# Attention, first round of batch 0: scores formed a second time, transposed, in place of 128-wide transposes of the exponentials

## The chip, the core and the metric

The kernel runs on one core of one Trainium2 chip, as one launch. The metric is the time of an execution on the device. A core has five engines that run side by side, each through its own list of instructions in order: PE (TensorE, products into PSUM), DVE (VectorE), ACT (ScalarE), POOL (GpSimd) and SP (SyncE, which here issues every DMA). They wait for each other through semaphores.

## The reference, cut to what matters

Sixteen pairs of heads (4 batches, 8 heads), 1152 keys and 64 values a head. Two neighbouring query rows are averaged, so 576 queries a head remain; then softmax attention, and on its output a bilinear layer in which two products of the same input are multiplied and sent through a third.

```python
q_pool = q.reshape(B, H, S // factor, factor, D).mean(axis=3)
scores = scale * np.matmul(q_pool, k.transpose(0, 1, 3, 2))
scores = scores - np.max(scores, axis=-1, keepdims=True)
attn = np.exp(scores)
attn = attn / (np.sum(attn, axis=-1, keepdims=True) + 1e-09)
attn_out = np.matmul(attn, v)
x = attn_out.transpose(0, 2, 1, 3).reshape(B * S, H * D)     # 2304 x 512
out = ((x @ w_a) * (x @ w_b)) @ w_out                        # 512 -> 1536 -> 512
```

## The kernel before

A pass takes one pair of heads (e = 0, 1) and some of their queries, in blocks of 128 queries by 1152 keys. Batch 0 goes in two rounds: first the "even" 256 queries of its four pairs (passes 0 to 3, four blocks each), then the "odd" 320 in reverse order (passes 4 to 7). Batches 1 to 3 take all 576 queries of a pair in one pass. Beside passes 0 to 3 the weights of the bilinear layer are prepared: 36 tiles are loaded, and each is taken apart into a large and a small half by ACT (`w_abs` L558, `w_tail` L577, `w_hi` L622), POOL (`w_sign` L581) and DVE (`w_join` L588, `w_lo` L626). The products of that layer (`moe_mm` L919, then `moe_o` L945) start when the first round of batch 0 is done and fill PE to the end of the program, between the blocks of later passes.

A block in passes 0 to 3, before: PE forms the scores (`qk` L682, two heads at a time in the two halves of the array's rows). DVE takes them from PSUM, negated, with their maximum (`sm_max` L717). ACT makes the exponentials with their sum (`sm_exp` L724). PE transposes them in 128x128 pieces (`tr_pe` L760) into the banks `ab0` and `ab1`, and ACT and DVE take turns to carry these to `pt` (`tr_out` L771, L773), read there as 32-bit numbers under the name `ptf`. PE multiplies with v (`pv_f` L804, two heads in the two halves of the array's columns). The reciprocal of the sum is spread by a diagonal matrix and a product with ones (`r_diag` L776, `r_wide` L780); `x_copy` L848 and `r_mul` L784 apply it. From pass 4 on a block goes another way: halves of 16 bits (`sm_hi` L737, `sm_lo` L741) and a DMA that transposes them into `pt` (L747); L838 multiplies with v.

The order of each engine's instructions is written out by hand: `ORDERS` lists the numbers of the tasks in the order in which `add` created them, one list an engine, and `Plan.order` only interleaves the five lists. The waits come from a tracker of what each instruction reads and writes in the tiles, whatever names the plan gave them.

## Time and profile before

| what | value |
|---|---|
| median of 3 runs | 839.35 us (837.95 to 842.45) |
| the profiled execution | 840.88 us, its span 839.1 us |
| busy share of the span | PE 93%, DVE 74%, ACT 69%, POOL 29% |
| mean granted TensorE clock | 0.981 |
| chain that ended last, by engine | PE 57%, DVE 2%, DMA 1% |

The span runs from the first to the last instruction. An engine is busy while an instruction runs; a clock of 1.00 is TensorE's upper level (2.4 GHz), its lower one is half of that. In a row of the timeline stand start, length, engine, line, operation, what is written and read, and in brackets the idle time before and what ended it. The length holds the tail of an instruction, under which the next one already runs, so the difference of two starts is the better measure in a dense stretch. Each 32-bit product shows as two matrix instructions (x10 is five products).

### The profile page before, as it was taken

Reading aid. Unit: us, or ns where it says so; the run is one execution under the profiler, and the core shown is the slowest. Engines: PE = TensorE matmul, PEld = TensorE weight load, DVE = VectorE, ACT = ScalarE, POOL = GpSimd, SP = SyncE. Lnnn points to the kernel's source line nnn. Section 1 sums busy time; section 2 is a strip of 40 time slices with the busy share of each in tenths; the row PEclk is TensorE's granted clock in tenths of the full one; section 3 lists DMA queues with packets and bytes.
Section 4 is the critical chain, followed back from the end, with each engine's and each line's share of the span. In section 5 each row is a group of like instructions: output and inputs, shape, how many; then the busy total and the mean of one; then the engine's idle time right before and its main releaser. Section 6 shows DMA issues by size and latency. Waiting matters only on the chain.

```text
span 839.1 us, 21333 instructions
## 1 busy us (share of the span) xinstructions
...
## 2 busy tenths in 40 slices
...
GB/s 262 208 188 204 208 144 192 211 199 196 209 212 210 195 200 189 232 173 217 192 185 211 182 206 194 164 171 173 151 127 127 127 30 128 13 26 1 27 2 25
DMA packets 316289, 132.32 MB, mean 158 GB/s; under 512 B 300832, under 2 KB 302880, under 8 KB 316192
## 3 DMA queue, kind: packets, MB, share of 16 engines
...
## 4 chain that ended last, share of the span: by engine, by line
PE 57%; DVE 2%; DMA 1%; ACT 0%; issue 0%
PE ab L919 26%; PE ab L945 15%; PE sps L685 8%; PE xps L838 8%; DMA pt<-p 1%; DVE p L741 1%; DVE s L717 1%; PE sps L682 0%; DVE g L931 0%; ACT g L926 0%; DVE o L951 0%; PE xps L496 0%; ACT p L737 0%; ACT s L724 0%; PE xps L429 0%
## 5 line engine op out<-in xcount | busy, mean ns | idle before, releaser
L919 PEld LDWEIGHTS <-wab 128*128 128x128 f16 x2592 | 252.2, 99 | 37.3 <-issue 6.3
L919 PE MATMUL ab<-xt,wab 128*128 128x256 f16 x2304 | 262.7, 274 | 2.7 <-DVE xt L881 0.9
L724 ACT ACTIVATE s<-s,st 128x1152 f32<-128x1152 f32 x144 | 179.9, 1250 | 34.5 <-DVE s L717 34.0
L939 POOL TENSOR_TENSOR gl<-g,gh 128x256 fp32r<-128x256 f32 x108 | 94.5, 880 | 358.1 <-ACT gh L936 349.7
L741 DVE SCALAR_TENSOR_TENSOR p<-s,st,p 128x1152 f16<-128x1152 f32 x128 | 181.5, 1424 | 10.0 <-ACT p L737 9.5
L737 ACT ACTIVATE p<-s,st 128x1152 f16<-128x1152 f32 x128 | 159.0, 1248 | 37.9 <-DMA pt<-p 13.3
L945 PE MATMUL ab<-wo,gh 128*128 128x512 f32 x432 | 139.8, 405 | 1.7 <-DVE g L931 1.7
L682 PE MATMUL sps<-k,q 64*128 64x512 f32 (+3 forms) x448 | 103.9, 557 | 22.6 <-DVE s L717 10.5
L926 ACT ACTIVATE g<-ab,cc 128x256 f32<-128x256 f32 (+1 forms) x144 | 55.4, 415 | 90.4 <-PE ab L919 90.3
L717 DVE TENSOR_SCALAR_CACHE_REDUCE s<-sps 128x1152 f32<-128x1152 f32 x72 | 96.7, 1350 | 25.7 <-PE sps L682 24.5
L717 DVE TENSOR_SCALAR_CACHE_REDUCE s<-sps,ksc 128x1152 f32<-128x1152 f32 x72 | 101.0, 1410 | 15.7 <-PE sps L685 15.3
L838 PE MATMUL xps<-pt,vs 128*64 128x128 f16 (+1 forms) x3888 | 109.3, 215 | 1.4 <-DMA pt<-p 1.1
L838 PEld LDWEIGHTS <-vs 128*64 128x64 f16 x3888 | 100.5, 110 | 13.5 <-issue 11.6
L931 DVE SCALAR_TENSOR_TENSOR g<-ab,cc,g 128x256 f32<-128x256 f32 (+1 forms) x144 | 55.2, 410 | 72.6 <-ACT g L926 72.6
L682 PEld LDWEIGHTS sps<-k,q 64*128 64x128 f32 (+1 forms) x448 | 48.5, 187 | 75.4 <-issue 52.4
L945 PEld LDWEIGHTS ab<-wo,gh 128*128 128x128 f32 x432 | 77.9, 188 | 20.4 <-ACT g L926 1.7
L945 PE MATMUL ab<-wo,gl 128*128 128x512 f32 x216 | 85.4, 395 | 0.0
L936 ACT ACTIVATE gh<-g 128x256 fp32r<-128x256 f32 x108 | 43.8, 411 | 54.8 <-PE ab L945 54.1
L685 PE MATMUL sps<-k,q 64*128 64x512 f16 (+3 forms) x624 | 65.5, 341 | 0.0
L685 PEld LDWEIGHTS <-q 64*128 64x128 f16 (+1 forms) x720 | 36.2, 97 | 39.6 <-issue 7.0
L581 POOL TENSOR_SCALAR xt<-xt 128x512 f16<-128x512 f32 x22 | 51.9, 2357 | 35.3 <-ACT xt L577 25.9
L419 POOL TENSOR_TENSOR q<-qraw 128x576 f32<-128x576 f32 (+2 forms) x20 | 25.0, 1250 | 92.3 <-PE sps L682 48.9
...
## 6 DMA issues: line engine op xcount, KB each, us to landing
...
```

The lines of the kernel that those rows point to most:

```text
L682: nc.tensor.matmul(out, q, k, start=True, stop=True)
L685: nc.tensor.matmul(out, q[:, hq], k[:, hk], start=(hq, hk) == (0, 0), stop=(hq, hk) == (1, 0))
L717: nc.vector.tensor_scalar(out=s_t[sbuf(i)], in0=sps[:, at:at + S], scalar1=-1.0 / 16.0 if u is None else ksc[:, u, 4:5], scalar2=None, op0 ...
L724: nc.scalar.activation(out=s, in_=s, func=AF.Exp, scale=-1.0, bias=t[:, 0:1], accum_out=t[:, 1:2])
L737: nc.scalar.activation(out=p_t[pbuf(i)][:, 0], in_=s_t[sbuf(i)], func=AF.Copy, scale=st_t[i % NST][:, 3:4])
L741: nc.vector.scalar_tensor_tensor(out=p[:, 1], in0=s, scalar=st_t[i % NST][:, 3:4], in1=p[:, 0], op0=ALU.mult, op1=ALU.subtract)
L838: nc.tensor.matmul(xps[half(e), at:at + w], vs[:, c, e, hv], pt[:, hp, c, c0:c0 + w], start=(c == 0 and n == 0), stop=(c == NCH - 1 and n ...
L919: nc.tensor.matmul(dst if t < 8 else dst.rearrange("p (b n) -> p b n", b=B), wab[:, f, 1 - m, a, c], moe_x(t, b, c), start=(n == 0), stop= ...
L926: nc.scalar.activation(out=g_t[:, f, c], in_=ab[j][:, 1, c], func=AF.Copy, scale=cc[:, b, f, 0:1])
L931: nc.vector.scalar_tensor_tensor(out=g, in0=ab[j][:, 0, c], scalar=cc[:, b, f, 1:2], in1=g, op0=ALU.mult, op1=ALU.mult)
L939: nc.gpsimd.tensor_tensor(out=gl_t[j], in0=g_t[:, f], in1=gh_t[j].bitcast(F32), op=ALU.subtract)
L945: nc.tensor.matmul(acc[u], g[:, us], wo[:, f, a], start=(first and n == 0), stop=(last and n == 2))
```

## The change

In passes 0 to 3 the blocks' scores are formed as before, but only for their maxima (`t_max`, a plain reduction). Four products with the identity lay the maxima of the 256 queries out as a row (`t_row`), which ACT copies (`t_keep`). Then the scores are formed again, transposed: keys on the partitions, 256 queries along the row, in five groups of two chunks of 128 keys (the last has one), and a second product subtracts the row of maxima (`t_s`). ACT makes the exponentials straight from PSUM into the place from which v is multiplied (`t_exp`): for passes 0 and 2 the buffers `p` and `s`, for 1 and 3 `pt`. `t_pv` multiplies with v, and by a product with ones also forms the sums, spread over the 64 rows of a head. `t_sum`, `t_rec` and `t_out` copy the sums, take their reciprocal and multiply. Diagonals, transposes and their copies are gone. `w_cc`, which scales the weights' factors, makes one instruction for four columns where there was one for each half column. All five lists of the order are new.

```diff
@@ -27,12 +27,13 @@
 P_SCALE = 2.0 ** 14
 
 REMN = 64
-N_PE, EVICT = 4, "ADADA"
+CC_F = 4
+N_PE = 4
 N_WHOLE, TWO_ROUNDS = 2, (0,)
 
 XE, XR, XO = 0, 256, 320
 
-S_AT = (0, 1408)
+S_AT, GAP = (0, 1408), 1152
 S_CUT = ((0, 512, 1024, 1152), (128, 640, 1152, 0, 128))
 TOK = 256
 
@@ -55,159 +56,154 @@
 
 ORDERS = (
     (
...
-        12, 18, 24, 26, 38, 28, 7, 30, 32, 44, 34, 35, 54, 56, 151, 58, 52, 60, 62, 157, 64, 65, 163, 177, 82, 167,
+        13, 15, 17, 19, 21, 8, 23, 133, 27, 26, 135, 31, 137, 35, 139, 30, 39, 141, 34, 38, 42, 143, 50, 253, 64, 147,
...
@@ -390,8 +387,19 @@
     kz = [z_t[2][:, 128 * j:128 * j + 128] for j in range(2)]
     kzf = [x.bitcast(F16).rearrange("p (a n) -> p a n", a=2) for x in kz]
 
-    ident, diag = g_t[:, 0, 0:128], [g_t[:, 1 + e, 0:128] for e in range(2)]
-    ptf = pt.rearrange("p a c n -> p (a c n)").bitcast(F32).rearrange("p (a c n) -> p a c n", a=2, c=NCH)
+    ident, sel = g_t[:, 0, 0:128], g_t[:, 1, 0:128]
+    mrow, rsum = [g_t[:, 2], g_t[:, 3]], g_t[:, 4]
+    GROUPS = [range(c, min(c + 2, NCH)) for c in range(0, NCH, 2)]
+    spare = [(x.rearrange("p a n -> p (a n)").bitcast(F32), [f"p{j}h", f"p{j}l"]) for j, x in enumerate(p_t)]
+    spare += [(x, [f"s{j}"]) for j, x in enumerate(s_t)]
+    spare = [(x[:, 512 * n:512 * n + 512], names) for x, names in spare for n in range(2)]
+    wide = pt.rearrange("p a c n -> p (a c n)").bitcast(F32)
+    wide = [(wide[:, 512 * n:512 * n + 512], [f"pt{j}" for j in range(NR)]) for n in range(9)]
+
+    def room(j, g, e):
+        n = 2 * g + e if g < 4 else 8
+        x, names = (spare, wide)[j][n]
+        return x[:, 256 * e:256 * e + 256] if g == 4 else x, names
     vf = [vs.rearrange("p c e h d -> p (c e h d)").bitcast(F32).rearrange("p (c n) -> p c n", c=NCH), vraw]
 
     def vbuf(p):
@@ -604,11 +613,10 @@
     def w_inv(f):
         nc.vector.reciprocal(out=wsc[:, 0, f], in_=wsc[:, 1, f])
 
-    def w_cc(f):
-        for m in range(2):
-            nc.vector.tensor_scalar(
-                out=cc[:, 0, f, m:m + 1], in0=wsc[:, 1, f, m:m + 1], scalar1=vb[:, 0, 0:1], scalar2=None, op0=ALU.mult
-            )
+    def w_cc(f0, f1):
+        nc.vector.tensor_scalar(
+            out=cc[:, 0, f0:f1], in0=wsc[:, 1, f0:f1], scalar1=vb[:, 0, 0:1], scalar2=None, op0=ALU.mult
+        )
 
     def w_dst(f, m, hl):
         return wab[:, f, m, hl] if m < 2 else wo[:, f, hl]
@@ -755,56 +763,87 @@
             out=ident, in_=ident, compare_op=ALU.not_equal, fill=1.0, base=0, pattern=[[-1, 128]], channel_multiplier=1
         )
 
-    def tr_pe(chunks, j):
...
-    def tr_out(chunks, j, on):
...
-    def r_diag(i, e):
...
-    def r_wide():
...
-    def r_mul(j, x0):
...
-    def moved(ps_, i0, u):
...
-    def pv_f(p, at, m):
...
+    def select():
+        nc.gpsimd.memset(sel, 0.0)
+        for e in range(2):
+            nc.gpsimd.memset(sel[64 * e:64 * e + 1], -1.0)
+
+    def t_max(i):
+        at = S_AT[blocks[i].head]
+        nc.vector.tensor_reduce(out=st_t[i % NST][:, 0:1], in_=sps[:, at:at + S], axis=AX.X, op=ALU.max)
+
+    def t_row(i0):
+        for r in range(2):
+            for e in range(2):
+                m = st_t[(i0 + 2 * r + e) % NST][:, 0:1]
+                nc.tensor.matmul(
+                    sps[half(e), GAP + 128 * r:GAP + 128 * r + 128], m.broadcast_to([128, 64]), ident, start=True, stop=True
+                )
+
+    def t_keep(j):
+        nc.scalar.activation(out=mrow[j], in_=sps[:, GAP:GAP + TOK], func=AF.Copy)
+
+    def t_s(ps_, j, g):
+        for n, c in enumerate(GROUPS[g]):
             for e in range(2):
                 nc.tensor.matmul(
+                    acc[e][:, TOK * n:TOK * n + TOK], kn[ps_.jk][half(e), 128 * c:128 * c + 128],
+                    qs[ps_.jq][half(e), 0:TOK], start=True, stop=False,
                 )
+            for e in range(2):
+                nc.tensor.matmul(acc[e][:, TOK * n:TOK * n + TOK], sel[half(e)], mrow[j][half(e)], start=False, stop=True)
+
+    def t_exp(j, g, e):
+        n = len(GROUPS[g])
+        nc.scalar.activation(
+            out=room(j, g, e)[0], in_=acc[e][:, 0:TOK * n], func=AF.Exp, scale=1.0 / 16.0
+        )
+
+    def t_pv(p, j, g):
+        at = [room(j, g, e)[0] for e in range(2)]
+        if g == 0:
+            for e in range(2):
+                nc.tensor.matmul(
+                    xps[half(e)], zero.broadcast_to([128, 64]), zero.broadcast_to([128, 2 * TOK]), start=True, stop=False
+                )
+        for n, c in enumerate(GROUPS[g]):
+            stop = c == NCH - 1
+            for e in range(2):
+                nc.tensor.matmul(xps[half(e), 0:TOK], vf[p % 2][:, c, 64 * e:64 * e + 64], at[e][:, TOK * n:TOK * n + TOK], start=False, stop=False)
+            for e in range(2):
+                nc.tensor.matmul(xps[half(e), TOK:2 * TOK], one.broadcast_to([128, 64]), at[e][:, TOK * n:TOK * n + TOK], start=False, stop=stop)
+
+    def t_sum():
+        nc.scalar.activation(out=rsum, in_=xps[:, TOK:2 * TOK], func=AF.Copy, bias=1e-9)
+
+    def t_rec():
+        nc.vector.reciprocal(out=rsum, in_=rsum)
+
+    def t_out(p, j, x0):
+        nc.vector.scalar_tensor_tensor(
+            out=x32[j][:, x0:x0 + TOK], in0=xps[:, 0:TOK], scalar=vsc[:, p, 0:1], in1=rsum, op0=ALU.mult, op1=ALU.mult
+        )
+
+    def t_pass(ps_, n):
+        j, i, p = n % 2, ps_.base, ps_.p
+        for rows, *_ in ps_.todo:
+            for e in range(2):
+                scores(ps_, i, rows, e)
+                ps_.last_max = add("DVE", 1.27, i - 4, t_max, (i,), r=[f"sps{e}"], w=[f"st{i % NST}m"])
+                i += 1
+        add("PE", 0.5, i - 10, t_row, (ps_.base,), r=[f"st{k % NST}m" for k in range(ps_.base, i)] + ["g0"], w=["gap"], mode=2)
+        add("ACT", 0.27, i - 4, t_keep, (j,), r=["gap"], w=[f"g{2 + j}"])
+        for g, of in enumerate(GROUPS):
+            w = len(of)
+            add("PE", 0.04 + 0.88 * w, i - 7 + g / 5, t_s, (ps_, j, g), r=kq_names(ps_) + ["g1", f"g{2 + j}"], w=["acc0", "acc1"], mode=1)
+            for e in range(2):
+                add("ACT", 0.06 + 0.21 * w, i - 4 + g / 5, t_exp, (j, g, e), r=[f"acc{e}"], w=[f"room{j}{g}{e}"])
+            add("PE", 0.04 + 0.88 * w + 0.25 * (g == 0), i - 9 + g / 5, t_pv, (p, j, g), r=[f"room{j}{g}{e}" for e in range(2)] + [x for e in range(2) for x in room(j, g, e)[1]] + vbuf(p) + ["ones"],
+                w=["xps"], mode=2)
+        add("ACT", 0.27, i - 5, t_sum, (), r=["xps"], w=["g4"])
+        add("DVE", 0.33, i - 5, t_rec, (), w=["g4"])
+        add("DVE", 0.4, i - 5, t_out, (p, ps_.jx, XE), r=["xps", "g4", f"vsc{p}"], w=[f"x32{ps_.jx}{c}" for c in range(XE // 64, (XE + TOK) // 64)])
+        x_split(ps_, ("even",), i - 4)
 
     def scores(ps_, i, rows, rest):
         whole = ps_.whole and rows[0][2] == 128
@@ -823,10 +862,6 @@
         add("ACT", 1.245, i - 3, sm_exp, (i,), r=[t + "m"], w=[s, t + "s"])
         add("DVE", 0.065, i - 5, sm_sum, (i,), r=[t + "s"], w=[t + "t"])
         add("DVE", 0.075, i - 5, sm_rec, (i,), r=[t + "t"], w=[t + "r"])
-        if ps_.pe:
-            e = blocks[i].head
-            add("ACT", 0.29, i - 3, r_diag, (i, e), r=[t + "r", "g0"], w=[f"g{1 + e}"])
-            return
         add("ACT", 1.15, i - 3.5, sm_hi, (i,), r=[s, t + "r"], w=[p + "h"])
         add("DVE", 1.37 if ps_.split else 1.4, i - 3, sm_lo, (i,), r=[s, p + "h", t + "r"], w=[p + "l"], port=True)
         add("SP", 2.97, i, transpose, (i,), r=[p + "h", p + "l"], w=[f"pt{slot}"], gen=0.42, block=1.02)
@@ -972,8 +1004,9 @@
             key = 1000 + 3 * len(steps)
             steps.append((t, f))
             scs = [f"cc{b}{f}" for b in bs]
-            if t == 0:
-                add("DVE", 0.14, -5, w_cc, (f,), r=[f"wsc{f}", "vb0"], w=[f"cc0{f}"])
+            if t == 0 and f % CC_F == 0:
+                of = range(f, f + CC_F)
+                add("DVE", 0.12, -5, w_cc, (f, f + CC_F), r=[f"wsc{x}" for x in of] + ["vb0"], w=[f"cc0{x}" for x in of], port=True)
             r = xs + [f"w{f}{m}{hl}" for m in range(2) for hl in "hl"]
             for m in range(2):
                 add("PE", 1.311, key + m, moe_mm, (t, f, m, j), r=r, w=[f"acc{j}"])
@@ -1081,8 +1115,12 @@
         nxt = passes[m + 1] if m + 1 < len(passes) else None
         if nxt:
             prep_qk(nxt, nxt.base - 6)
+        if ps_.pe:
+            t_pass(ps_, m)
+            if nxt and not nxt.again:
+                prep_vmax(nxt.p, nxt.parts[0] == "even", ps_.end - 4)
         i = ps_.base
-        for r, (rows, (at, w), leaving, splits) in enumerate(ps_.todo):
+        for r, (rows, (at, w), leaving, splits) in enumerate(ps_.todo if not ps_.pe else ()):
             slots = []
             for n in range(2 if w == 128 else 1):
                 slots.append(blocks[i].slot)
@@ -1091,14 +1129,7 @@
                 i += 1
             if r == 1 and nxt and not nxt.again:
                 prep_vmax(nxt.p, nxt.parts[0] == "even", ps_.end - 4)
-            if ps_.pe:
-                parts = moved(ps_, i - 2, r)
-                add("PE", 2.02, i - 10, pv_f, (ps_.p, at, 64 * slots[0]), r=[f"pt{t}" for t in slots] + parts + vbuf(ps_.p),
-                    w=["xps"], mode=2)
-                add("PE", 0.3, i - 10, r_wide, (), r=["g1", "g2", "ones"], w=["xps"], mode=2)
-                leaving = [(at, XE + at, 128)]
-            else:
-                unit(slots, at, w, i - 1)
+            unit(slots, at, w, i - 1)
             for span in leaving:
                 leave(ps_, *span, i - 1)
             if splits:
```

PE at the start of the program, before: `sps` holds the scores, `ab0` and `ab1` the two banks, `s0` and `s1` the exponentials, `g` the identity.

```order
L682 MATMUL sps_99<-k1_69,q0_73 128x128 x2
L760 MATMUL ab0_100<-g_84,s0_75 128x128 x4
L760 MATMUL ab1_101<-g_84,s0_75 128x128 x4
L682 MATMUL sps_99<-k1_69,q0_73 128x512 x4
L682 MATMUL sps_99<-k1_69,q0_73 128x128
L760 MATMUL ab0_100<-g_84,s1_76 128x128 x4
L496 MATMUL xps_102<-vmx_93,one_92 128x2
L760 MATMUL ab1_101<-g_84,s1_76 128x128 x4
```

The same place now (`st` holds the maxima; `g` in L779 is the identity, in L794 the row of maxima):

```order
L690 MATMUL sps_100<-k1_69,q0_73 128x512 x4
L690 MATMUL sps_100<-k1_69,q0_73 128x128 x2
L779 MATMUL sps_100<-g_84,st_80 64x128 x4
L504 MATMUL xps_103<-vmx_94,one_92 128x2
L789 MATMUL ab0_101<-q0_73,k1_69 128x256
L789 MATMUL ab1_102<-q0_73,k1_69 128x256
L794 MATMUL ab0_101<-g_84 128x256
```

The transposes that stood between the first two pairs of score blocks are gone; the transposed scores stand behind the maxima of all four blocks.

PE at the end of the first round, before, up to the first product of the bilinear layer (L919; `xt0` its input):

```order
L804 MATMUL xps_102<-pt_67,vraw_71 64x128 x18
L780 MATMUL xps_102<-g_84,one_92 64x128 x2
L682 MATMUL sps_99<-k1_69,q1_74 128x128
L919 LDWEIGHTS wab_61
L919 MATMUL ab0_100<-xt0_63,wab_61 128x256
```

The same place now (L812 and L814 are `t_pv`, L690 scores of pass 5, L951 is `moe_mm`):

```order
L812 MATMUL xps_103<-pt_67,vraw_71 64x256 x2
L814 MATMUL xps_103<-pt_67,one_92 64x256 x2
L690 MATMUL sps_100<-k1_69,q1_74 64x512 x4
L690 MATMUL sps_100<-k1_69,q1_74 64x128 x2
L690 MATMUL sps_100<-k1_69,q1_74 128x512 x4
L690 MATMUL sps_100<-k1_69,q1_74 128x128
L951 LDWEIGHTS wab_61
L951 MATMUL ab1_102<-xt0_63,wab_61 128x256
```

The scores of pass 5 have moved behind the last product with v; the first product of the bilinear layer still stands behind both.

DVE there, before (L717 and L728 belong to blocks of the odd round, L784 is `r_mul`, L881 scales the layer's input):

```order
L626 SCALAR_TENSOR_TENSOR wab_61<-o0_89,wsc_97,wab_61 128x512
L717 TENSOR_SCALAR s1_76,st_80<-sps_99 128x1152
L588 SCALAR_TENSOR_TENSOR z2_91<-z2_91,g_84 128x512
L609 TENSOR_SCALAR cc_98<-wsc_97,vb_95 128x1 x2
L784 SCALAR_TENSOR_TENSOR x32_66<-x32_66,xps_102 128x128
L728 TENSOR_SCALAR st_80<-st_80 128x1
L881 TENSOR_SCALAR xt0_63<-xt0_63,vsc_94 128x2x256
```

And now (L725 is `sm_max`, L749 `sm_lo`, L820 and L823 are `t_rec` and `t_out` of pass 3, L913 scales the layer's input):

```order
L725 TENSOR_SCALAR s2_77,st_80<-sps_100 128x1152
L596 SCALAR_TENSOR_TENSOR o1_90<-o1_90,wab_61 128x512
L749 SCALAR_TENSOR_TENSOR p0_81<-s0_75,st_80,p0_81 128x1152
L820 RECIPROCAL g_84<-g_84 128x256
L913 TENSOR_SCALAR xt0_63<-xt0_63,vsc_95 128x2x256
L823 SCALAR_TENSOR_TENSOR x32_66<-xps_103,vsc_95,g_84 128x256
L634 SCALAR_TENSOR_TENSOR wab_61<-o0_89,wsc_98,wab_61 128x512
L736 TENSOR_SCALAR st_80<-st_80 128x1
L725 TENSOR_SCALAR s0_75,st_80<-sps_100 128x1152
```

The reciprocal of pass 3 stands between two maxima of the odd round.

SP at the first DMA transposes, before (L552 loads a tile of weights, L411 and L414 load k and q):

```order
L747 DMA_TRANSPOSE pt_67<-p1_82 128x18x128
L552 DMA wab_61<-in_w_out_dram 128x1024
L411 DMA k0_68<-in_k_dram 128x1152
L552 DMA xt1_64<-in_w_ab_dram 128x1024
L414 DMA qraw_70<-in_q_dram 128x2x320
L552 DMA xt1_64<-in_w_out_dram 128x1024
L552 DMA g_84<-in_w_ab_dram 128x1024
L747 DMA_TRANSPOSE pt_67<-p2_83 128x18x128
```

And now (L560, L419 and L422 are these loads):

```order
L419 DMA k0_68<-in_k_dram 128x1152
L560 DMA xt1_64<-in_w_ab_dram 128x1024
L422 DMA qraw_70<-in_q_dram 128x2x320
L755 DMA_TRANSPOSE pt_67<-p1_82 128x18x128
L755 DMA_TRANSPOSE pt_67<-p2_83 128x18x128
L560 DMA xt1_64<-in_w_ab_dram 128x1024
L755 DMA_TRANSPOSE pt_67<-p0_81 128x18x128
L560 DMA xt1_64<-in_w_out_dram 128x1024
```

Before, ten of the 36 loads of weights stood behind the first transpose; now five do, and the transposes follow each other more closely.

## Rows read from the trace of the kernel before

**Rows 1.** Stages of the program: stretch, length, each engine's busy time (instructions), TensorE's clock.

```profile
26.55:60.00 33.45, 26.55 (x237) 19.30 (x238) 31.43 (x66) 32.88 (x71) 22.27 (x12) 1.00 0.53 190
60.00:98.00 38.00, 27.73 (x199) 18.23 (x196) 34.26 (x85) 36.17 (x72) 27.28 (x15) 0.91 0.59 202
98.00:132.00 34.00, 16.48 (x112) 11.49 (x112) 24.80 (x49) 22.84 (x42) 20.81 (x11) 0.70 0.58 169
132.00:180.00 48.00, 43.88 (x599) 34.55 (x599) 42.72 (x89) 43.37 (x73) 18.97 (x12) 0.99 0.95 205
300.00:700.00 400.00, 396.56 (x5123) 308.78 (x5121) 342.06 (x637) 298.63 (x459) 82.11 (x97) 1.00 0.91 169
0.00:132.00 132.00, 89.22 (x646) 60.50 (x646) 104.40 (x229) 107.79 (x211) 85.49 (x50) 0.90 0.59 200
```

**Rows 2.** Timeline of PE, end of the first round (start, length, what, idle before).

```profile
106.46 0.59 PE L597 MATMUL xps<-wmx,one 128*128 128x2 f32 x2 [7.42 <-ACT wab L567]
109.93 4.11 PE L682 MATMUL sps<-k,q 64*64 64x512 f32 x12 [2.88 <-issue]
...
117.05 3.44 PE L804 MATMUL xps<-pt,vraw 128*64 128x128 f32 x36 [0.96 <-DVE wsc L600]
...
127.59 3.72 PE L804 MATMUL xps<-pt,vraw 128*64 128x128 f32 x36 [4.38 <-DVE x L784]
...
132.00 1.16 PE L919 MATMUL ab<-xt,wab 128*128 128x256 f16 x9
```

**Rows 3.** Timeline of ACT in the same stretch.

```profile
102.69 0.45 ACT L771 ACTIVATE pt<-ab 128x128 f32<-128x128 f32 x2 [4.09 <-DMA pt<-p]
```

**Rows 4.** Timeline of DVE in the same stretch.

```profile
125.14 0.69 DVE L773 COPY pt<-ab 128x512 f32<-128x512 f32 x1 [3.57 <-DMA pt<-p]
```

**Rows 5.** Timeline of PE: the start, a dense stretch, and one at half clock.

```profile
5.88 4.18 PE L682 MATMUL sps<-k,q 64*128 64x512 f32 x10 [5.88 <-DMA k<-in_k_dram]
...
14.86 4.15 PE L682 MATMUL sps<-k,q 64*128 64x512 f32 x10
...
21.06 2.19 PE L804 MATMUL xps<-pt,vs 128*64 128x128 f32 x36
23.07 0.39 PE L780 MATMUL xps<-g,one 128*64 128x128 f32 x4
23.39 1.09 PE L760 MATMUL ab<-g,s 128*128 128x128 f32 x8
24.42 2.20 PE L682 MATMUL sps<-k,q 64*128 64x512 f32 x10
26.55 0.66 PE L760 MATMUL ab<-g,s 128*128 128x128 f32 x4
...
68.36 4.21 PE L682 MATMUL sps<-k,q 64*128 64x512 f32 x10
...
77.57 2.15 PE L682 MATMUL sps<-k,q 64*64 64x512 f32 x12 [1.44 <-DVE s L717]
```

**Rows 6.** Timeline of DVE, the first maxima.

```profile
10.09 1.36 DVE L717 TENSOR_SCALAR_CACHE_REDUCE s<-sps 128x1152 f32<-128x1152 f32 x1 [10.09 <-PE sps L682]
```

**Rows 7.** Groups by line and form, 0 to 132.1: busy time, mean ns of one, idle before.

```profile
L724 ACT ACTIVATE s<-s,st 128x1152 f32<-128x1152 f32 x22 | 27.6, 1255 | 1.1 <-DVE s L717 1.1
...
L773 DVE COPY pt<-ab 128x512 f32<-128x512 f32 x16 | 10.8, 680 | 3.9 <-DMA pt<-p 3.6 <-PE ab L760 0.4
...
L771 ACT ACTIVATE pt<-ab 128x512 f32<-128x512 f32 x16 | 9.5, 591 | 3.1 <-PE ab L760 3.0
...
L776 ACT ACTIVATE g<-g,st 128x128 f32<-128x128 f32 x16 | 6.3, 398 | 1.4 <-DVE st L734 1.4
...
L734 DVE RECIPROCAL st<-st 128x1 f32<-128x1 f32 x21 | 3.3, 166 | 0.0
...
L728 DVE TENSOR_SCALAR st<-st 128x1 f32<-128x1 f32 x21 | 3.0, 143 | 0.0
...
L605 DVE RECIPROCAL wsc<-wsc 128x2 f32<-128x2 f32 x9 | 1.5, 162 | 0.1
```

47 lines of the change are left out of this document (7 added, 40 removed), and 283 rows, old and new, of the table ORDERS.

## The prediction

> **What bounds the kernel now.** I read the stages first, since the page's shares (PE 93%) are a mean over very different stretches. From 300 to 700 us PE is busy 396.56 of 400 us [rows 1]: there only PE work counts, and the change leaves that work alone. From 0 to 132.0 it is busy 89.22 us, and at 132.00 the first product of the bilinear layer starts [rows 1, 2]. After it the same instructions remain to be done in both kernels, so the question is when this product starts.
>
> Within the first 132 us there are two regimes. From 26.55 to 60 DVE and ACT are full (31.43 and 32.88 of 33.45 us) and PE is idle for 6.9 us, 21% [rows 1]. From 98 to 132 nobody is full: PE 16.48, DVE 24.80, ACT 22.84, POOL 20.81 of 34 us, at a mean clock of 0.70 [rows 1]. The timeline shows why: ACT's copy of a transposed piece into `pt` waits 4.09 us for a DMA that fills `pt` with the odd round's blocks, and DVE's 3.57 us in the same way [rows 3, 4]; PE waits 7.42 and 4.38 us behind them [rows 2]. In these idle stretches PE falls to half its clock: the same 36 instructions that take 2.19 us take 3.44 and 3.72 [rows 2, 5].
>
> So I split PE's 132.0 us into work at full clock, work lengthened by the low clock, and idle time. Three times five score products took 4.18, 4.15 and 4.21 us where 2.20 is the full-clock length, twelve instructions 4.11 where it is 2.15, and two products with v 1.3 and 1.5 us more than 2.19 [rows 2, 5]: 10.8 us. Short pieces of the same stretches add about 3 (an estimate from their share). That leaves 89.2 - 13.8 = 75.4 us of work; 13.8 + 42.8 us are lost.
>
> **The change, part by part.** PE. Two heads side by side count as one step. Five score products (512, 512 and 128 columns a head pair or head) take 26.55 - 24.42 = 2.13 us, 1.85 ns a column; nine steps of 128 columns with v take 23.07 - 21.06 = 2.01 us, 1.745 ns a column [rows 5]. A step of 256 columns is then 0.473 us in `t_s`, which uses row halves as the scores do, and 0.447 us in `t_pv`, which uses column halves. Each has 18 steps a pass: 8.5 and 8.0 us. The zeroing product (16-bit, 512 columns) is about 0.26 us (9 products of 256 columns last 1.16 us [rows 2]), the row of maxima two steps of 128 columns, 0.45. Added: 17.2 us a pass. Removed: 36 transposes at 1.03/8 = 0.129 us, twice 2.01 us with v, twice 0.32 us of spreading (23.39 - 23.07) [rows 5]: 9.3 us. Net +7.9 us a pass, 32 us in four; bounds 30 (all steps at 0.447) and 35 (all at 0.473, and 0.1 us more at each group's change of halves).
>
> ACT, per pass: four exponentials of 1.255 us, four diagonals of 0.398 and four copies of 0.591 go, eight exponentials of 512 columns come [rows 7]. I price these as the copy of the same shape from PSUM, 0.591; two of 256 columns and the two small copies stand against the small copies that go. 9.0 - 4.7 = 4.3 us less, 17 us in four passes. DVE: four copies of 0.680 and eight short ones of some 0.15 us go [rows 7]; a reciprocal and a multiplication of 256 columns come, 0.45 us each; the maxima cost what they did. 3.0 us less a pass, 12 in four. `w_cc` issues 3 instructions in place of 24, at 0.143 us or less [rows 7]: up to 3 us of DVE. With 107.8 - 17 = 91 us of ACT, 104.4 - 15 = 89 of DVE, 85.5 of POOL and 75.4 + 32 = 107.4 of PE before the first bilinear product [rows 1], PE becomes the longest, and what DVE and ACT save is worth only what PE's waits shrink.
>
> The two waits for DMA go: the plan now knows `pt` as a buffer that passes 1 and 3 read, and the transposes wait until pass 3 is done. What is late instead is said under the third rival. The tiles k and q now stay in use until a pass's last transposed scores, so the loads of k and q for the pass after next, the weights behind them in SP's queue and POOL's sum of q start later; PE asks for them a whole pass later, which hides them, and if it does not, one landing of a load is lost, within the upper bound of the waits below. POOL's and DVE's small fills at the start lie beside the first loads: nothing.
>
> **The start.** PE's first scores still start at 5.88 and end at 10.06, at half clock; DVE's maxima follow at 10.09, 1.3 us each with a piece of scores between them [rows 5, 6]. Now PE has nothing else: the second pair of blocks can start at about 14.0, lasts 4.15 at half clock, two more maxima and a piece between them take it to 21.7, the row of maxima and its copy to 23.3, and the first group of `t_s` at half clock to 26.5. By then 7.4 us of full-clock work is done: 19.1 us are lost, all hidden by nothing.
>
> **The sum.** 107.4 + 19.1 = 126.5 us if PE then never waited. Break-even with 132.0 is therefore 5.5 us of waits in 100 us of PE work. What I expect:
> - Both banks are taken by a group of `t_s`, so the next group needs both exponentials (2 x 0.59 and two hand-overs). Mostly other products stand between; at six places only a short one does, 0.6 us each: 3.5.
> - The sums come back through ACT, two DVE instructions and hand-overs in some 1.9 us; PE covers that with the next pass's first group (1.9): 0. If that cover went, it would be 1.9 us a pass.
> - At the end of the round PE's scores for passes 4 and 5 wait for DVE's maxima, which stand behind halves, weights, the reciprocal and the multiplication: 1.6 and 2.6, in all 4.2.
> - The last exponentials of pass 3 stand on ACT behind the odd round's exponential of 1.255 us [rows 7]: 1.2.
>
> Together 8.9 us. The bounds are 3 (the third item alone, in part) and 21 (the 21% of idle PE between 26.55 and 60 carried over 100 us); I stay below the middle since DVE and ACT have lost a sixth of their load. The first bilinear product then starts at 135.4, 3.4 us later. PE's gaps after 132 (4.1 us up to 180, 3.4 from 300 to 700 [rows 1]) I leave as they are; the odd round is a little further behind on DVE, so -3 to +4 us. The profiled execution took 840.88 us, so 844.3; it lay 1.5 us above the median, so 842.8 against 839.35. Forecast 843.
>
> **The rivals.** (1) *PE is never starved.* DVE and ACT end with 40 us to spare in 132, the clock stays at its upper level, and the waits stay under 4 us: 834 to 838, say 836. For it speak the spare time and the end of the DMA waits; against it, that each queue runs in order, and that PE already waited 21% of a stretch in which no DMA held it up. (2) *The wide reciprocal is slow.* A reciprocal of one element lasts 0.166 us, a scaling of one 0.143 [rows 7]: were the 23 ns the price of an element, 256 would cost 5.9 us; the one of two elements (0.162) shows no growth at all, which I take. At the middle, 2.5 us more each, the reciprocals of passes 2 and 3, which stand before maxima that PE needs, and that of pass 0, whose cover is used up, give 6 us: 849, slower, from 0.5 us more on. The Trainium skill, VectorE: DVE Perf Modes, section "First, the fixed hardware budget", says that a reciprocal is an iterative divide with a repeat count of 8; with the 0.96 GHz of its "Specifications" that would be an estimated 2.1 us for 256 columns, and 848 by the same places. No row here has a wide one, and the row with two elements does not agree. (3) *The last weights come late.* The first DMA transpose waits for the last product of pass 3, and five loads of weights stand behind it, some behind transposes that need the odd round's halves. If two of these (some 3.5 us each) come before the last factors and PE has run out, 849. Against it: before, ten loads stood behind the first transpose. (4) *Heads don't run side by side* in the new products: 144 steps of 0.45 us more, 904. The dense rows show that they do for scores and for v [rows 5].
>
> **How the numbers follow.** The forecast, with waits of 5 to 12 us, gets 0.45 (838.5 to 846); rival 1 0.27, rival 2 0.13, rival 3 0.13, rival 4 0.02. A measurement tells about 0.5% (4.2 us) from no change, so faster means under 835.2: most of rival 1, 0.24. Same, up to 843.5: the rest of it and two thirds of the forecast, 0.35. Slower: 0.41. The range from 833 to 853 leaves out the fast end of rival 1, the slow ends of 2 and 3, and 4.
>
> **What would show it.** First bilinear product (L951) at 135 (132 or less: rival 1). PE's work at full clock before it near 107 us; a granted clock of 1.00 from 27 us on. No wait for a DMA into `pt` on ACT or DVE. L820 at 0.45 us, not 2 or more. PE's longest waits on the maxima at the end of the round. Wrong in kind would be PE idle above 15 us between 27 and 135 us, or a new gap after 140 us behind the weights' sums (L606).

## The result, and the profile after

The changed kernel takes 851.22 us (median of 4 runs, 850.14 to 852.72) against 839.65 of the kernel before (837.95 to 842.45). The ratio is 1.0136, with a 95% interval from 1.0103 to 1.0168: 11.6 us slower. The forecast was 843, slower by 3.4, in a range from 833 to 853. The direction was right; the forecast size was about a third of what came.

Where the time went is read by stages, as before. This is the changed kernel over the stretches of [rows 1] (time, then busy time and instructions of PE, PE's weight loads, DVE, ACT and POOL, then the granted clock, the DMA share and GB/s):

```profile
0.00:26.55 26.55, 14.50 (x52) 8.68 (x54) 9.57 (x14) 7.07 (x13) 11.37 (x15) 0.74 0.64 237
26.55:60.00 33.45, 32.42 (x248) 22.28 (x246) 20.60 (x28) 19.01 (x37) 16.40 (x10) 1.00 0.37 125
60.00:98.00 38.00, 36.54 (x278) 24.57 (x277) 28.83 (x45) 31.53 (x63) 30.73 (x16) 0.96 0.57 199
98.00:132.00 34.00, 29.48 (x214) 18.69 (x212) 32.15 (x57) 31.11 (x54) 25.26 (x14) 0.95 0.59 199
300.00:700.00 400.00, 393.47 (x5109) 305.38 (x5104) 346.12 (x637) 299.05 (x455) 90.09 (x98) 1.00 0.93 170
0.00:139.00 139.00, 116.73 (x796) 75.89 (x796) 98.15 (x156) 94.24 (x175) 88.92 (x55) 0.91 0.57 189
```

From 26.55 to 60 the roles are exchanged: PE, which was idle for a fifth of this stretch, is nearly full (32.42 of 33.45 us), and DVE and ACT, which were full, work 20.60 and 19.01 us. From 98 to 132 DVE is at 95%, and PE is busy for 29.48 us where it was for 16.48. PE's own timeline (start, duration, line, tiles, count, and in brackets the idle time before it and what ended that) at the places that matter:

```profile
6.25 3.63 PE L690 MATMUL sps<-k,q 64*128 64x512 f32 x10 [6.25 <-DMA k<-in_k_dram]
...
13.27 4.20 PE L690 MATMUL sps<-k,q 64*128 64x512 f32 x10 [1.45 <-DVE st L773]
...
22.73 1.22 PE L789 MATMUL ab<-q,k 64*128 64x256 f32 x4
...
49.06 0.35 PE L504 MATMUL xps<-vmx,one 128*128 128x2 f32 x2 [1.03 <-DVE x L823]
49.34 2.20 PE L690 MATMUL sps<-k,q 64*128 64x512 f32 x10
...
113.76 0.70 PE L789 MATMUL ab<-q,k 64*128 64x256 f32 x4 [2.41 <-ACT pt L798]
...
115.19 3.79 PE L690 MATMUL sps<-k,q 64*128 64x512 f32 x10
...
135.21 3.90 PE L690 MATMUL sps<-k,q 64*128 64x512 f32 x10 [4.28 <-DVE s L725]
139.03 2.79 PE L951 MATMUL ab<-xt,wab 128*128 128x256 f16 x24
...
353.52 0.38 PE L504 MATMUL xps<-vmx,one 128*128 128x2 f32 x2 [2.64 <-DVE vmx L500]
353.76 1.05 PE L977 MATMUL ab<-wo,gh 128*128 128x512 f32 x2
...
359.29 0.63 PE L977 MATMUL ab<-wo,gh 128*128 128x512 f32 x2
```

L951, the first bilinear product, starts at 139.03, where it started at 132.00 [rows 2]. So 7.0 us of the span's 10.9 (850.0 less 839.1) are lost before it. The other 3.9 come after it: the largest place is at 353 us, where PE waits 2.64 us for a maximum of v and then runs at half clock for a while (1.05 us for a pair of products that takes 0.63 at 359; the mean granted clock from 353.52 to 356.40 is 0.57). DVE forms this maximum at 352.11, after a wait for the load of v, which SP issues late:

```profile
346.98 0.52 SPq L416 DMA_DIRECT2D vraw<-in_v_dram  x1
```

This split rests on one profiled execution of each kernel. From the first bilinear product to the end it is 711.0 us here and 707.1 before; in the seven experiments below that keep the changed kernel's order it is 708.6 to 710.6, so this part costs 1.5 to 3.9 us.

The new operations, grouped by line and shape up to 140 us (count, then busy us, mean ns of one, idle time of the engine before them):

```profile
L789 PE MATMUL ab<-q,k 64*128 64x256 f32 x144 | 28.4, 431 | 2.4 <-ACT pt L798 2.4
L814 PE MATMUL xps<-pt,one 128*64 128x256 f32 x72 | 10.9, 379 | 0.0
L798 ACT ACTIVATE pt<-ab 128x512 f32<-128x512 f32 x16 | 9.2, 590 | 4.7 <-PE ab L794 4.6
L820 DVE RECIPROCAL g<-g 128x256 f32<-128x256 f32 x4 | 7.0, 1746 | 6.1 <-ACT g L817 6.1
L773 DVE TENSOR_REDUCE st<-sps 128x1 f32<-128x1152 f32 x16 | 21.6, 1352 | 21.7 <-PE sps L690 21.7
```

The exponentials cost what was forecast (0.590 us against 0.591), and the wide reciprocal 1.746 us where 0.45 was taken. On DVE it stands in the queue of the round's end like this:

```profile
129.50 1.41 DVE L749 SCALAR_TENSOR_TENSOR p<-s,st,p 128x1152 f16<-128x1152 f32 x1
130.83 1.74 DVE L820 RECIPROCAL g<-g 128x256 f32<-128x256 f32 x1
132.49 0.25 DVE L913 TENSOR_SCALAR xt<-xt,vsc 128x512 f16<-128x512 f16 x1
132.67 0.48 DVE L823 SCALAR_TENSOR_TENSOR x<-xps,vsc,g 128x256 f32<-128x256 f32 x1
133.07 0.74 DVE L634 SCALAR_TENSOR_TENSOR wab<-o,wsc,wab 128x512 f16<-128x512 f32 x1
133.73 0.15 DVE L736 TENSOR_SCALAR st<-st 128x1 f32<-128x1 f32 x1
133.79 1.35 DVE L725 TENSOR_SCALAR_CACHE_REDUCE s<-sps 128x1152 f32<-128x1152 f32 x1
```

No row here has idle time before it. The maximum (L725) at 133.79 is the one for which PE waits 4.28 us, and it waits behind everything above, the reciprocal included. PE's last scores then run at half clock (3.90 us where the same ten instructions take 2.20 at 49.34; the mean granted clock from 135.21 to 139.10 is 0.56).

The waits for a DMA into `pt` [rows 3, 4] are gone: the waits of ACT and DVE up to 140 us hold none.

### The profile page after: what moved, and what is told of

It is laid out like the page before. It is cut to its first block, busy times and chain, and to the rows that moved or that the text cites. A ratio compares the mean times of both kernels' runs of the same rounds, so it can differ in the third digit from the quotient of the medians.

```text
span 850.0 us, 21505 instructions
## 1 busy us (share of the span) xinstructions
PE 809.3 (95%) x9016; PEld 620.1 (73%) x9016; DVE 617.6 (73%) x1131; ACT 565.1 (66%) x946; POOL 255.8 (30%) x229
## 4 chain that ended last, share of the span: by engine, by line
PE 51%; DVE 7%; DMA 3%; ACT 1%; issue 1%; POOL 0%; SPq 0%; ACTq 0%
PE ab L951 22%; PE ab L977 15%; PE sps L693 7%; PE xps L873 6%; DVE p L749 3%; DMA pt<-p 2%; DVE s L725 2%; ACT p L745 1%; DVE g L963 1%; PE sps L690 1%; DMA vraw<-in_v_dram 1%; DVE vs L537 0%; DVE vmx L500 0%; DVE kmx L430 0%; ACT s L732 0%
## 5 line engine op out<-in xcount | busy, mean ns | idle before, releaser
L951 PEld LDWEIGHTS <-wab 128*128 128x128 f16 x2592 | 251.1, 98 | 33.8 <-issue 3.6
L951 PE MATMUL ab<-xt,wab 128*128 128x256 f16 x2304 | 260.9, 273 | 2.3 <-DVE g L963 1.5
L971 POOL TENSOR_TENSOR gl<-g,gh 128x256 fp32r<-128x256 f32 x108 | 102.7, 956 | 321.2 <-ACT gh L968 275.9
L749 DVE SCALAR_TENSOR_TENSOR p<-s,st,p 128x1152 f16<-128x1152 f32 x128 | 182.7, 1431 | 22.8 <-ACT p L745 22.0
L732 ACT ACTIVATE s<-s,st 128x1152 f32<-128x1152 f32 x128 | 159.7, 1248 | 27.5 <-DVE s L725 26.8
L690 PE MATMUL sps<-k,q 64*128 64x512 f32 (+3 forms) x448 | 102.1, 549 | 19.5 <-DVE s L725 7.3
L725 DVE TENSOR_SCALAR_CACHE_REDUCE s<-sps,ksc 128x1152 f32<-128x1152 f32 x72 | 100.8, 1411 | 8.4 <-PE sps L693 7.9
L690 PEld LDWEIGHTS sps<-k,q 64*128 64x128 f32 (+1 forms) x448 | 48.7, 186 | 72.4 <-issue 53.7
L725 DVE TENSOR_SCALAR_CACHE_REDUCE s<-sps 128x1152 f32<-128x1152 f32 x56 | 75.2, 1349 | 2.3 <-PE xps L814 0.9
L589 POOL TENSOR_SCALAR xt<-xt 128x512 f16<-128x512 f32 x22 | 55.0, 2500 | 29.1 <-ACT xt L585 21.4
L427 POOL TENSOR_TENSOR q<-qraw 128x576 f32<-128x576 f32 (+2 forms) x20 | 26.9, 1344 | 73.4 <-DMA qraw<-in_q_dram 39.8
```

What stands on the lines that cost most here:

```text
L690: nc.tensor.matmul(out, q, k, start=True, stop=True)
L725: nc.vector.tensor_scalar(out=s_t[sbuf(i)], in0=sps[:, at:at + S], scalar1=-1.0 / 16.0 if u is None else ksc[:, u, 4:5], scalar2=None, op0 ...
L732: nc.scalar.activation(out=s, in_=s, func=AF.Exp, scale=-1.0, bias=t[:, 0:1], accum_out=t[:, 1:2])
L749: nc.vector.scalar_tensor_tensor(out=p[:, 1], in0=s, scalar=st_t[i % NST][:, 3:4], in1=p[:, 0], op0=ALU.mult, op1=ALU.subtract)
L951: nc.tensor.matmul(dst if t < 8 else dst.rearrange("p (b n) -> p b n", b=B), wab[:, f, 1 - m, a, c], moe_x(t, b, c), start=(n == 0), stop= ...
L971: nc.gpsimd.tensor_tensor(out=gl_t[j], in0=g_t[:, f], in1=gh_t[j].bitcast(F32), op=ALU.subtract)
```

## The experiments

Each was timed against the kernel before on the same chip (medians from 840.1 to 840.7 us there). "Won" is the difference of its ratio to 1.0136, in us. Each ratio is uncertain by 0.2 to 0.5%, that is by 2 to 4 us, and 1.0136 by 0.33%, so what was won is uncertain by some 3.5 to 5 us: a gain of 6 us is clear of zero, one of 2 us is not. "First product" is the start of the first bilinear product in us, from one profiled run; how much it varies from run to run was not measured. Passes are counted from 1 in this section, so pass 1 is pass 0 of the plan.

| experiment | median us | ratio, 95% interval | won | first product |
|---|---|---|---|---|
| changed kernel | 851.22 | 1.0136 [1.0103, 1.0168] | | 139.0 |
| e1 short reciprocal | 845.83 | 1.0066 [1.004, 1.0093] | 5.9 | 132.4 |
| e2 no ones | 848.96 | 1.0114 [1.0071, 1.0158] | 1.8 | 136.1 |
| e3 short maxima, pass 1 | 844.94 | 1.0059 [1.0037, 1.0082] | 6.5 | 133.2 |
| e4 short maxima, passes 2 to 4 | 850.91 | 1.013 [1.008, 1.018] | 0.5 | 139.7 |
| e5 changed, reordered | 847.58 | 1.0064 [1.0018, 1.011] | 6.0 | 135.3 |
| e6 before, reordered, no DMA waits | 832.09 | 0.9901 [0.9863, 0.9939] | | 123.5 |
| e7 sums from PSUM | 850.38 | 1.0116 [1.0078, 1.0153] | 1.7 | 137.9 |
| e8 = e1 and e2 | 844.54 | 1.0049 [1.0024, 1.0075] | 7.3 | 131.9 |
| e9 scores of 128 keys | 843.26 | 1.0045 [1.0016, 1.0074] | 7.6 | 131.3 |
| e10 = e9, reordered | 832.32 | 0.9898 [0.9865, 0.9931] | 20 | 111.8 |
| e11 before, reordered, DMA waits left | 841.79 | 1.0023 [0.9998, 1.0048] | | 135.1 |

### e1: the reciprocal

```diff
-        nc.vector.reciprocal(out=rsum, in_=rsum)
+        nc.vector.tensor_scalar(out=rsum, in0=rsum, scalar1=2.0 ** -10, scalar2=None, op0=ALU.mult)
```

> The changed kernel with the wide reciprocal (L820) replaced by a multiplication with a constant of the same shape; the division by the sums is left out. It should last about 0.45 us in place of 1.75, so DVE is rid of 4 x 1.3 = 5.2 us, two of the four in the stretch from 98 to 139 us, where DVE is busy 95% of the time. Theory (DVE is the bound at the end of the first round): both lie on the path, first bilinear product 2.6 us earlier (136.4 in place of 139.0), the whole 3 to 5 us less, about 847. Rival (the loss is PE's own work and the half clock, the reciprocal is covered): first product within 0.7 us of 139.0, whole 850 to 851.

This leaves out the division by the sums. The instruction in its place takes 0.502 us on average (0.67, 0.76, 0.29 and 0.29 in the four passes). Its group row, and PE's last scores with the first product in this kernel:

```profile
L820 DVE TENSOR_SCALAR g<-g 128x256 f32<-128x256 f32 x4 | 2.0, 502 | 6.1 <-ACT g L817 6.1
```
```profile
130.25 2.20 PE L690 MATMUL sps<-k,q 64*128 64x512 f32 x10 [2.89 <-DVE s L725]
132.38 1.16 PE L951 MATMUL ab<-xt,wab 128*128 128x256 f16 x9
```

4 x 1.24 = 5.0 us of DVE gave 5.9 us of the whole (3 to 5 were expected, which the uncertainty doesn't exclude), and the first product comes 6.6 us earlier (2.6 were expected): three of the four reciprocals lie on the path, not two. One sees it in a chain that has nothing to do with sums, POOL's part of the weights (L589). Five of its instructions, first of the changed kernel, then of this one:

```profile
44.03 2.25 POOL L589 TENSOR_SCALAR xt<-xt 128x512 f16<-128x512 f32 x1 [5.70 <-ACT xt L585]
...
62.93 2.26 POOL L589 TENSOR_SCALAR xt<-xt 128x512 f16<-128x512 f32 x1 [2.87 <-ACT xt L585]
...
90.80 2.29 POOL L589 TENSOR_SCALAR g<-g 128x512 f16<-128x512 f32 x1
...
118.69 2.59 POOL L589 TENSOR_SCALAR wab<-wab 128x512 f16<-128x512 f32 x1
...
134.44 2.25 POOL L589 TENSOR_SCALAR g<-g 128x512 f16<-128x512 f32 x1
```
```profile
43.92 2.25 POOL L589 TENSOR_SCALAR xt<-xt 128x512 f16<-128x512 f32 x1 [5.70 <-ACT xt L585]
...
61.58 2.29 POOL L589 TENSOR_SCALAR xt<-xt 128x512 f16<-128x512 f32 x1 [2.69 <-ACT xt L585]
...
87.27 2.29 POOL L589 TENSOR_SCALAR g<-g 128x512 f16<-128x512 f32 x1
...
115.13 2.60 POOL L589 TENSOR_SCALAR wab<-wab 128x512 f16<-128x512 f32 x1
...
129.75 2.25 POOL L589 TENSOR_SCALAR g<-g 128x512 f16<-128x512 f32 x1
```

They come 0.1, 1.4, 3.5, 3.6 and 4.7 us earlier. Between one and the next stands one of the four reciprocals (46.6, 72.9, 105.5 and 130.8 in the changed kernel): the first, second and fourth each leave a step, the third none. The second's step (2.2 us) is larger than the instruction: PE no longer falls to half clock behind it (granted clock 1.00 from 60 to 98, where it was 0.96). At the end the last scores take 2.20 us in place of 3.90, which gives most of the step from 4.7 to 6.6. A long instruction in a queue that runs in order pushes everything behind it, weights and maxima alike.

### e2 and e8: the product with ones

```diff
             for e in range(2):
-                nc.tensor.matmul(xps[half(e), 0:TOK], vf[p % 2][:, c, 64 * e:64 * e + 64], at[e][:, TOK * n:TOK * n + TOK], start=False, stop=False)
-            for e in range(2):
-                nc.tensor.matmul(xps[half(e), TOK:2 * TOK], one.broadcast_to([128, 64]), at[e][:, TOK * n:TOK * n + TOK], start=False, stop=stop)
+                nc.tensor.matmul(xps[half(e), 0:TOK], vf[p % 2][:, c, 64 * e:64 * e + 64], at[e][:, TOK * n:TOK * n + TOK], start=False, stop=stop)
...
-        nc.scalar.activation(out=rsum, in_=xps[:, TOK:2 * TOK], func=AF.Copy, bias=1e-9)
+        nc.scalar.activation(out=rsum, in_=xps[:, TOK:2 * TOK], func=AF.Copy, bias=1024.0)
```

> The changed kernel without the product of the exponentials with ones (L814); the sums it divides by are then a constant. It takes 9 x 4 x 0.43 = 15.5 us of full-clock work from PE before the first bilinear product and nothing from any other engine. If PE's work is the bound all along, the first bilinear product comes 13 to 15.5 us earlier and the whole is 836 to 838. If the backlog of weights on DVE and ACT decides, PE only waits more: the first product 3 to 7 us earlier, the whole 844 to 848, with PE idle 8 to 12 us more before it.

The gain came out as small as the second reading had it, and smaller: the first product 2.9 us earlier where that had 3 to 7, the whole 848.96 where it had 844 to 848. Two stretches of this kernel, in the columns of the stages above:

```profile
98.00:132.00 34.00, 23.65 (x122) 13.36 (x122) 31.84 (x58) 29.49 (x52) 23.14 (x14) 0.80 0.61 186
0.00:132.00 132.00, 103.88 (x642) 65.88 (x642) 93.98 (x148) 90.19 (x169) 85.05 (x54) 0.90 0.57 192
```

PE has less to do, waits instead, and falls to half clock more often (mean 0.80 from 98 to 132, where it was 0.95). From 26.55 to the first product it is idle for 16.6 us, where it was for 10.2, and busy for 92.9 where it was for 102.3: of the 15.5 us taken away 6.4 became waiting, some 6 went into a lower clock (the rest of the sum), and 2.9 came through. PE's sum of work is not what bounds this round.

e8 joins the two edits.

> The changed kernel without the product with ones and with the reciprocal replaced by a multiplication with a constant: the first two experiments in one (apart they gave 6.0 and 1.9 us). If PE's queue and DVE's queue run side by side as two paths of nearly one length, the two gains add up to more than their sum: first bilinear product at 126 to 129, whole 839 to 842. If each is a place on one path, they add up: 129.5 (139.0 less 6.6 less 2.9), whole 843 to 844.

The first product came at 131.9, hardly before e1's 132.4 and later than both readings had it, and the whole won 7.3 us, about the sum (7.7). My reading of PE's and DVE's queues as two parallel paths of equal length fell: with the reciprocal short, 15.5 us of PE work still won only 1.4 us more, uncertain by some 3.

### e3, e4 and e9: the start

```diff
-        nc.vector.tensor_reduce(out=st_t[i % NST][:, 0:1], in_=sps[:, at:at + S], axis=AX.X, op=ALU.max)
+        at, n = S_AT[blocks[i].head], 128 if i < 4 else S
+        nc.vector.tensor_reduce(out=st_t[i % NST][:, 0:1], in_=sps[:, at:at + n], axis=AX.X, op=ALU.max)
```

e4 has `i >= 4` in its place: the other twelve.

> The changed kernel with the maxima of the first pass taken over 128 of the 1152 columns. The four maxima last some 0.25 us in place of 1.36, and at the start PE waits for each of them: first transposed scores at 18.5 in place of 22.73. Theory (the start delays the weights as well as PE, and all that follows): 4 us earlier is kept to the first bilinear product (135) and to the end, whole 846 to 847. Rival (only the end of the round decides): PE waits longer there, first product 0 to 1.5 us earlier, whole 850 to 851.

> The changed kernel with the maxima of passes 2 to 4 (not the first) taken over 128 of the 1152 columns: 12 x 1.1 = 13 us less of DVE between 28 and 89 us. If DVE's backlog is what holds the end of the round, its weights get done earlier, DVE has idle time from 98 to 139, and the first bilinear product comes 4 to 7 us earlier, whole 844 to 847. If PE's work and its start decide, only PE's short waits on these maxima go (0.8 us): first product within 1.5 us, whole 849.5 to 851.

The four of pass 1 won 6.5 us, the twelve of the others 0.5. For the first that is more than the 4 us expected, and for the others it is what the second reading had. The start of e3 on PE:

```profile
10.67 0.48 PE L690 MATMUL sps<-k,q 64*128 64x128 f32 x2 [0.38 <-DVE st L773]
...
16.90 0.89 PE L789 MATMUL ab<-q,k 64*128 64x256 f32 x4
```

The transposed scores start at 16.90, 5.83 us earlier, and the first bilinear product 5.9 us earlier: what the start loses is not made up anywhere before it. That DVE does 12 us less up to 132 in e4 (this row, against 91.15 in the changed kernel) shows no gain; the first product comes 0.7 us later, and the whole can't be told from the changed kernel's:

```profile
0.00:132.00 132.00, 113.76 (x786) 74.67 (x786) 78.79 (x143) 87.66 (x164) 82.98 (x52) 0.92 0.54 186
```

The start holds up more than PE. SP issues its loads in order, and the loads of weights (L560) wait until DVE has worked off a buffer (SP's waits up to 140 us: total, times, longest):

```profile
SPq L560 <- DVE o L596: 39.0, 8, 9.7
```

In the changed kernel SP issues nothing between these two rows, 14.6 us apart, while DVE's queue goes through the maxima; the buffer `xt` is free when L596, behind the fourth maximum, has read it (21.03 to 21.71):

```profile
7.16 0.49 SPq L416 DMA_DIRECT2D vraw<-in_v_dram  x1
21.73 0.33 SPq L560 DMA_DIRECT2D xt<-in_w_ab_dram  x1
```

e3 issues that load at 16.67.

e9 takes the maxima of all four passes over 128 keys and forms no other scores in the first round.

```diff
     def qk(ps_, rows, rest):
+        if ps_.pe:
+            for e in range(0 if rest else 2):
+                c, at = rows[e][1], S_AT[e]
+                product(sps[:, at:at + 128], None, qs[ps_.jq][half(e), c:c + 128], kn[ps_.jk][half(e), 0:128])
+            return
```

> The changed kernel in its own order, with the maxima of all four passes taken over the scores of the first 128 keys alone (softmax is the same for any shift; what is given up is the guard against overflow by the other 1024 keys), so that the scores of the other keys are not formed in the first round. Takes about 18 us of PE work, 18 us of DVE and most of the half-clock start. Theory (the start is on the path, PE's work is not): the start gives about 10 us more than the maxima of pass 1 alone gave, in all first bilinear product at 127 to 131, whole 839 to 843. If PE's added work were what counts, the 18 us of PE would come on top: first product at 112 to 118, whole 825 to 831.

```profile
15.37 1.12 PE L784 MATMUL sps<-g,st 128*64 128x128 f32 x8 [7.03 <-DVE st L778]
...
127.87 3.46 PE L690 MATMUL sps<-k,q 64*128 64x512 f32 x10 [3.98 <-DVE s L730]
131.26 3.18 PE L956 MATMUL ab<-xt,wab 128*128 128x256 f16 x24
```

It came out just beyond the slow end of the first theory (131.3 and 843.26, where that had 127 to 131 and 839 to 843), far from the second: the start is now a wait of 7.03 us for DVE, whose queue has weights ahead of the last maxima, and the round's end waits for DVE (3.98 us) as before. Again some 18 us of PE work and 17 of DVE's won hardly more than the start alone (7.6 against e3's 6.5).

### e5, e6, e10 and e11: the orders

In these the five lists of the queues' order were searched anew, by trying moves of single entries against a schedule with measured durations (the code's own list gives the reciprocal 0.33 us). The instructions stay. e6 also holds the DMA transposes back:

```diff
-                add("ACT" if on == "A" else "DVE", ..., tr_out, (chunks, j, on), r=[f"acc{j}"], w=[name])
+                moved_ids.append(add("ACT" if on == "A" else "DVE", ..., tr_out, (chunks, j, on), r=[f"acc{j}"], w=[name]))
...
-        add("SP", 2.97, i, transpose, (i,), ..., gen=0.42, block=1.02)
+        add("SP", 2.97, i, transpose, (i,), ..., gen=0.42, block=1.02, after=moved_ids)
```

> The changed kernel with the same instructions, but the orders of the five queues written anew, with the durations that the runs so far showed (above all the reciprocal at 1.7 us, which the order in the code takes as 0.33). Theory (the loss sits in waits along queues that run in order: the four reciprocals, the start, DVE's queue from 104 to 135 us): first bilinear product 7 to 9 us earlier than 139.0, whole 840 to 844. Rival (the added work itself is the loss, in whatever order): first product within 3 us, whole 847 to 851.

> The kernel before, its queues written anew in the same way, and its DMA transposes made to wait until the last copy of a transposed piece into pt, so that no copy waits for a DMA (the two waits of 4.09 and 3.57 us go). If the waits for DMA into pt were what the change had to win, this alone should win it: first bilinear product at 118 to 124 in place of 132.0, whole 829 to 834. If the old form of the first round is bound by ACT's and DVE's work (107.8 and 104.4 of 132 us), little changes: first product 128 to 132, whole 836 to 840.

> The kernel before, its queues written anew as in the sixth experiment, but without making the DMA transposes wait, so that the copies into pt can still be caught behind a DMA. If the gain of the sixth (8.6 us) was the end of those two waits, this one stays within 2 us of the kernel before, 838 to 842, with waits for a DMA into pt of 3 us or more on ACT or DVE. If it was the new order, this one is as fast as the sixth, 831 to 834.

e6 won 0.99% on the kernel before, as expected, e11 nothing, with the same search. What differs by intent is the waits for DMA into `pt`. In e11 one is left on ACT, a little under the 3 us expected, and PE has long waits later (a row of ACT, then two of PE):

```profile
107.17 0.45 ACT L753 ACTIVATE pt<-ab 128x128 f32<-128x128 f32 x2 [2.79 <-DMA pt<-p]
```
```profile
117.54 3.92 PE L786 MATMUL xps<-pt,vraw 128*64 128x128 f32 x36 [1.96 <-DVE wsc L582]
126.24 4.11 PE L786 MATMUL xps<-pt,vraw 128*64 128x128 f32 x36 [4.56 <-DVE wab L608]
```

The second of these is a wait for a DMA into `pt` too, though the row names DVE: the last copy by DVE into `pt` began at 119.52, and PE goes on when this transpose has landed, by the trace at 126.10, 4.6 us after its issue:

```profile
121.52 2.75 SPq L729 DMA_TRANSPOSE pt<-p  x1
```

In e6 there is none on ACT, DVE or PE, and the first product comes at 123.5. Holding the transposes back, with an order searched for it, was thus worth some 10 us against the search alone (0.9901 against 1.0023, uncertain by some 4 us). It isn't shown that the two waits of e11, 2.79 and 4.56 us, are all of this: its other queues differ from e6's too. And the one-line rule in the old order, without a new search, was not run, so what it is worth alone stays open.

e5 won about 6 us, less than the 7 to 11 expected, and is uncertain: its six runs lie between 839.28 and 851.11, and the profiled one is the slowest. By its ratio, 1.0064, it is still slower than the kernel before.

> The same, with the five queues written anew for it with measured durations. If what is left after the experiment before is waiting along the queues, most of it goes: first bilinear product at 113 to 119, whole 826 to 834, about level with the reordered kernel before (832). If the search only fits its own durations, as in part with the first reordered kernel: 836 to 842.

e10, at 832.32 us, is level with e6, as expected. Its first product comes at 111.8, earlier than any and than expected, yet the whole is no shorter: what follows takes 720.4 us, against 711.0 in the changed kernel, with PE idle for 23.9 us of it against 18.4. So with a new order this start is no longer a measure of the whole; the table's last column compares only kernels of one order.

### e7: the copy of the sums

```diff
-        nc.scalar.activation(out=rsum, in_=xps[:, TOK:2 * TOK], func=AF.Copy, bias=1e-9)
-        nc.vector.reciprocal(out=rsum, in_=rsum)
+        nc.vector.reciprocal(out=rsum, in_=xps[:, TOK:2 * TOK])
```

> The changed kernel with the reciprocal reading the sums from PSUM; ACT's copy of them (L817, 0.38 us, four times) and its 1e-9 are left out. At the end of pass 4 that copy starts 1.7 us after the last product, behind an exponential of 1.25 us. Theory (the path runs product, copy, reciprocal, multiplication in passes 1, 2 and 4): 0.4 to 0.6 us in each of passes 1 and 2 is won; in pass 4 DVE is busy anyway until 130.8. First bilinear product 0.5 to 1.5 us earlier, whole 849.5 to 850.5. Rival (the copy is covered): no change, 851.

The first product came 1.1 us earlier, as the theory had it. The whole won 1.7 us by the ratios, which can't be told from nothing.

## Why the prediction was right or wrong

**Right in kind.** The waits for `pt` went; the start lost what was forecast (first transposed scores at 22.73, with 14.50 us of mostly half-clock work by 26.55, the mean granted clock 0.74); products and exponentials cost what their neighbours' rows said; heads run side by side. PE's longest wait after the start is on the maxima at the round's end. Weights that come late behind the transposes, the third rival, show no wait of PE above 0.4 us. From 26.55 to 139 PE is idle for 112.45 - (116.73 - 14.50) = 10.2 us, where 8.9 were forecast, though in other items: the exponentials cost 2.4 (one wait) and not 3.5 and 1.2, the return of the sums 1.4 and not 0, the maxima 5.1 (0.8 and 4.3) and not 4.2, and four short waits 1.3.

**Wrong in size: the reciprocal.** The step "a reciprocal and a multiplication of 256 columns come, 0.45 us each" took its price from an element count of two, where no growth can be seen. The reciprocal is 1.746 us. I had set that as a rival of 0.13, with 2.5 us more at each of three places (7.5 us), put at 6 in all. The price was 1.3 us more and not 2.5. Three was the right number of places, but one of them was wrong: I had named passes 0, 2 and 3, and it was 0, 1 and 3 (the first, second and fourth). With the half clock that goes too, e1 measured 5.9 us, so that the rival's 6 came out by a price too high and a clock that it didn't count. Forecast and this rival together give 849. The Trainium skill, VectorE: DVE Perf Modes, section "First, the fixed hardware budget", names an iterative divide with a repeat count of 8, from which, with the clock in its "Specifications", I had estimated 2.1 us. The trace, 1.746 us, lies between that estimate and the rows I followed, much nearer to the estimate.

**Wrong: the clock.** "A granted clock of 1.00 from 27 us on" didn't hold: 0.96 from 60 to 98 and 0.95 from 98 to 132. Ten score products take 3.79 us at 115.19 and 3.90 us at 135.21 in place of 2.20, the granted clock being 0.58 and 0.56 there, each time after PE had been idle for 2.4 or 4.3 us shortly before. That is 3.3 us which the sum had at zero; a third such place, at 77.28 to 81.00 (0.54), comes on top.

**At the slow edge: after the first bilinear product.** I left this part as it was, with -3 to +4 us for the odd round. It takes 3.9 us more in the profiled run, 1.5 or more in every kernel of this order. The order of the later passes was written anew as well, and at 353 us PE waits for a v whose load SP issues only at 347. I had not followed the queues that far.

**Errors that cancel.** In e1 the reciprocal's place costs about what the forecast had for it (0.50 us). Yet the first bilinear product then comes at 132.4, 3.0 us before the forecast's 135.4, and the part behind it lasts 2.7 us longer than before (709.8 against 707.1). So with that price the whole, 845.83, lies near the forecast only because two other terms cancel: work and waits before that product that were put too high (PE is idle for 7.0 us from 26.55 to it, where 8.9 were forecast), and a loss behind it that was put at nothing.

**Wrong in its ground: "PE becomes the longest".** The sum added PE's work and took the rest as waits. It came near since the waits were sized to the old stretches, but PE's work is not the bound: 15.5 us less of it won 1.8 (e2), 1.4 more beside e1 (e8). DVE's sum doesn't look like the bound either: 12 us less won 0.5 (e4), though this is uncertain by 5. What fits the runs, though it was not followed from end to end, is a path that goes through the queues in turn: the maxima of the start, then the products of the first pass, the sums' return, and DVE's queue from 104 us on. 5.0 us taken off four instructions of it won 5.9 (e1), 4.3 at its head won 6.5 (e3); both intervals lie wholly below the changed kernel's.

**What the change won and lost.** The old form, with the transposes held back and reordered, runs at 832 us; with the waits left, a reordering won nothing. So a gain of 1% was to be had without the new products. Compared on equal terms, each without these waits and with an order searched for it, the new form (e5, 1.0064) is some 14 us slower than the old (e6, 0.9901), uncertain by some 5. It is level with it when most of the first scores are left out (e10, 0.9898), so in reordered kernels forming the scores twice costs about what the new form loses. In the order of the change, the reciprocal costs about 6 us and the maxima of the start about as much. Together that is the size of the loss of 11.6 us, but the two were not taken out in one run, and how the loss splits between these, the half clock and the later passes was not measured one by one.
